# Fixing the order of TensorE, VectorE and ScalarE in a sliding-window attention

## The chip, the cores and the metric

The kernel runs on one core of one Trainium2 chip. The metric is the device time of one execution in microseconds (us); lower is better. The runs of one kernel agree within 1.5%. A profile covers one execution. Engine names: PE is TensorE, DVE is VectorE, ACT is ScalarE, POOL is GpSimd.

## The reference, cut to what matters

One transformer block on 2048 tokens of width 512: a modulated LayerNorm, attention with 32 heads of width 16 in which a query sees the 256 keys up to its own, an output projection, two more LayerNorms, and an MLP across tokens.

```python
mask = (idx[:, None] - idx[None, :] >= 0) & (idx[:, None] - idx[None, :] < W)   # W = 256
scores = jnp.where(mask[None, None], scores, -1000000000.0)
p = _softmax(scores, axis=-1)
o = jnp.einsum('bhqk,bhkd->bhqd', p, v)
...
h = _layernorm(x, axis=-1) * (1 + ca) + sa
x = x + ga * _A_ref(h, A_wqkv, A_wo)          # attention
h = _layernorm(x, axis=-1) * (1 + cb) + sb
x = x + gb * _B_ref(h, B_w1, B_b1, B_w2, B_b2)   # MLP across tokens
```

## The kernel before

Tokens are handled in four groups of 512, and the heads of a group in four units of 8. A unit has five chunks (four in group 0). A chunk is: scores on PE into `pss`, one exp on ACT from `pss` to `et`, two mask multiplications on DVE, then the value sums on PE: `pox` collects the weighted values, `poy` the normalisers. After a unit's last chunk ACT computes 1/poy as exp(-ln(poy)), and DVE scales: `OT = pox * lz`. There are 76 chunks in all. Beside them runs "dense" work: the projections of the next group, the output projection and LayerNorms of the previous group, and in groups 2 and 3 the first halves ("partials") of MLP sums.

The tiles into which PE writes its results are in PSUM, and the program has few of them. `pss` (128 x 2048) exists once, so the next scores wait for this exp (7.0 us in 14 waits of the profiled run). `pox` and `poy` exist once each, so a new unit's first value sums wait for the scaling of the unit before (up to 1.2 us at a time there). Dense jobs share two buffers of 128 x 512 (`ps_d`). To copy a result out of PSUM is called an eviction here; it is done by DVE, or by ACT as a "side job" beside its exps. In the profiled run one of 128 x 512 took 0.68 us on DVE (`kb`, mean) and 0.58 to 0.60 us on ACT (`QT`).

```python
    ps_d = ctx.enter_context(tc.tile_pool(name="ps_d", bufs=2, space=PSUM))
    ps_s = ctx.enter_context(tc.tile_pool(name="ps_s", bufs=1, space=PSUM))
    ps_o = ctx.enter_context(tc.tile_pool(name="ps_o", bufs=1, space=PSUM))
    ...
    def emit_norm(u):
        lz = work.tile([P, D], F32, name="lz", tag="lz", bufs=2)
        nc.scalar.activation(out=lz[:], in_=u.y[:], func=ACT.Ln)
        nc.scalar.activation(out=lz[:], in_=lz[:], func=ACT.Exp, scale=-1.0)
        nc.vector.tensor_tensor(out=OT[u.G % 2][u.g8][:], in0=u.x[:], in1=lz[:], op=ALU.mult)
    ...
        et = emit_exp_mask(tiles, ch, mk)
        if i + 1 < len(steps):
            v = steps[i + 1][0]
            tiles = emit_scores(v.G, v.g8, steps[i + 1][2])
        pend.append((u, ci, ch, et))
        credit += per_step
        while bg and credit >= 1.0:          # dense jobs of this chunk
            bg.pop(0)()
            credit -= 1.0
        while len(pend) > (1 if i + 1 < len(steps) else 0):
            pu, pci, pch, pet = pend.pop(0)
            emit_av(pu, pci, pch, pet, pci == 4)
            if pci == 4:
                emit_norm(pu)
```

This is only the order in which the program is written. A scheduler puts each engine's instructions into another order at build time. The order that each engine then ran is read from the profiles.

The softmax here doesn't subtract the row's maximum and nothing guards it: scores larger than these inputs give would overflow.

## Time and profile before

The median is 333.14 us (332.96 to 334.24, three runs). The profiled run took 331.52 us.

| part of the profiled run (span 329.7 us) | us |
|---|---|
| start of the 1st and of the 2nd exp | 24.65, 32.62 |
| group 0, from its 2nd exp | 38.8 |
| groups 1, 2, 3 | 55.2, 55.7, 53.3 |
| end of the last exp | 235.6 |
| from there to the end (MLP) | 94.1 |
| time in the attention at half clock (2 us windows) | 10 |

The group times are differences of exp starts in the ScalarE timeline; the last group ends with its last exp. The half-clock time is the missing clock summed over windows of 2 us and doubled, since 0.50 is the lowest clock that any of these windows shows.

The page of the profile, with busy time and share of each engine, then the busy tenths of PE in 40 slices, the granted clock in tenths, and the shares of the chain of waits:

```profile
PE 256.8 (78%) x3269; PEld 125.8 (38%) x3313; DVE 227.3 (69%) x517; ACT 182.6 (55%) x165; POOL 34.8 (11%) x68
...
PE   0588888987876756986789796888873899999973
...
PEclk9999999999999995899999999999997899999999
...
PE 37%; DVE 35%; ACT 15%; DMA 8%; issue 3%; SPq 1%; another core or an unknown queue 0%; DVEq 0%; ACTq 0%
```

No engine is saturated (PE, the busiest, has 78%), and the chain passes from one engine to another. Whoever wants to gain time here has to shorten waits, not work.

The list of waits (who waited for whom: us in total, times, longest):

```profile
ACT et L413 <- PE pss L401: 34.6, 49, 1.6
...
PE pox L465 <- DVE et L425: 13.3, 21, 1.3
...
PE pox L465 <- DVE OT_1_147 L478: 1.6, 2, 1.2
```

ACT loses 34.6 us waiting for scores. PE waits 13.3 us in one of the groups for masks before value sums. Waits of `pox` for a scaling `OT` are small: the one shown is the largest of eight groups, and the eight sum to 5.2 us.

The timeline, in order of start (start, duration, engine, line, operation; in brackets the idle time before and its end):

```profile
113.98 1.88 ACT L413 ACTIVATE et<-pss 128x2048 bf16<-128x2048 f32 x1 [0.50 <-PE pss L401]
...
115.76 0.59 ACT L476 ACTIVATE lz<-poy 128x512 f32<-128x512 f32 x1
...
116.38 0.63 ACT L477 ACTIVATE lz<-lz 128x512 f32<-128x512 f32 x1
...
116.92 1.86 ACT L413 ACTIVATE et<-pss 128x2048 bf16<-128x2048 f32 x1
117.04 0.69 DVE L478 TENSOR_TENSOR OT_2_152<-pox,lz 128x512 bf16<-128x512 f32 x1
...
117.78 0.41 PE L465 MATMUL pox<-et,VT_143 128*32 128x192 bf16 x12 [0.22 <-DVE OT_2_152 L478]
...
119.27 1.88 ACT L413 ACTIVATE et<-pss 128x2048 bf16<-128x2048 f32 x1 [0.50 <-PE pss L401]
...
121.20 0.40 PE L401 MATMUL pss<-QT_3_130,KT_3_138 32*128 32x192 bf16 x8 [1.12 <-ACT et L413]
...
121.65 1.88 ACT L413 ACTIVATE et<-pss 128x2048 bf16<-128x2048 f32 x1 [0.50 <-PE pss L401]
...
123.58 0.40 PE L401 MATMUL pss<-QT_3_130,KT_3_138 32*128 32x128 bf16 x12 [1.26 <-ACT et L413]
```

Two steady rhythms are seen. Between plain chunks, exps start 2.38 us apart (119.27 to 121.65): 1.88 us of exp, then 0.50 us in which PE makes the next scores. Where ACT also makes a normaliser it is 2.94 us (113.98 to 116.92). There DVE does the scaling at 117.04, as soon as the normaliser is there.

Windows of 4 us (length, then busy time of PE, PEld, DVE, ACT, POOL, each with its count; granted clock, DMA share, GB/s):

```profile
120.00:124.00 4.00, 1.53 (x40) 0.94 (x37) 1.07 (x4) 3.03 (x2) 0.00 (x0) 1.00 0.00 0
124.00:128.00 4.00, 2.38 (x52) 1.44 (x53) 0.81 (x3) 3.26 (x2) 0.00 (x0) 0.55 0.00 0
```

From 120 us there is no dense work and PE is busy 1.53 of 4 us. After that the granted clock falls: 0.55 in the window from 124 us, and 0.50 in the 2 us windows from 126 to 134 us. In the 8 us ahead of the fall PE had no gap above 1.26 us: low activity without a long gap came before it.

### The profile page before, as it was taken

To read this page: it belongs to the slowest core of one execution; us is meant where nothing else is said; L and a number is where in the kernel's file an instruction comes from. 1 tells how busy PE (TensorE), PEld (TensorE's weight loads), DVE (VectorE), ACT (ScalarE), POOL (GpSimd) and SP (SyncE) were. 2 spreads that over 40 slices of the span, in tenths; PEclk is the share of its full clock that TensorE was granted. 3 is DMA by queue.
4 is the path that set the end of the run, shared out by engine and by line. 5 is a ranking of instruction groups with operands and counts; after the bars stand their busy time and mean duration, and the time that the engine had idled before them with its cause. 6 is when DMAs were issued, how large, how long until landed. Compare 5 with 4: busy or idle time off the path is not lost.

```text
span 329.7 us, 7582 instructions
## 1 busy us (share of the span) xinstructions
PE 256.8 (78%) x3269; PEld 125.8 (38%) x3313; DVE 227.3 (69%) x517; ACT 182.6 (55%) x165; POOL 34.8 (11%) x68
## 2 busy tenths in 40 slices
PE   0588888987876756986789796888873899999973
PEld 0353435343543423453344343433331344444431
DVE  7999988648899543899955689644387476535433
ACT  1014797987868788786888876878602353000000
POOL 8403101230101400020230000000000000000000
PEclk9999999999999995899999999999997899999999
DMA  7992039300000000000002202222200991110110
GB/s 219 336 334 6 3 85 287 79 2 0 4 2 2 2 2 2 2 2 1 2 2 66 66 2 66 64 67 66 67 0 10 398 412 73 51 48 34 62 34 32
DMA packets 31434, 24.62 MB, mean 75 GB/s; under 512 B 6056, under 2 KB 29608, under 8 KB 31400
## 3 DMA queue, kind: packets, MB, share of 16 engines
q1 hardware_dynamic: 30336, 23.08, 22.8%
q10 hardware_dynamic: 1064, 1.05, 1.1%
q8 instruction: 26, 0.43, 0.5%
q14 instruction: 8, 0.07, 0.1%
HBM read 22.03 MB, written 2.10 MB: 73 GB/s over the span
## 4 chain that ended last, share of the span: by engine, by line
PE 37%; DVE 35%; ACT 15%; DMA 8%; issue 3%; SPq 1%; another core or an unknown queue 0%; DVEq 0%; ACTq 0%
ACT et L413 11%; DVE st L243 6%; PE pu_4802 L649 4%; PE pu_4645 L649 4%; PE pu L442 4%; DVE et L420 4%; PE pss L401 3%; PE pox L465 3%; DVE et L425 3%; PE pu_4257 L592 2%; DMA x_73<-in_A_x_dram 2%; DMA wqkv<-in_A_wqkv_dram 2%; PE pu_4484 L592 2%; DMA b2b<-in_B_b_dram 2%; DVE VT_143 L336 2%
## 5 line engine op out<-in xcount | busy, mean ns | idle before, releaser
L413 ACT ACTIVATE et<-pss 128x2048 bf16<-128x2048 f32 (+1 forms) x76 | 140.6, 1851 | 35.2 <-PE pss L401 34.6
L465 PE MATMUL poy<-et,ones_bd 128*32 128x128 bf16 (+4 forms) x768 | 42.9, 256 | 4.7 <-DVE et L420 3.5
L420 DVE TENSOR_TENSOR et<-et,maskt 128x256 bf16<-128x256 bf16 (+2 forms) x104 | 32.9, 338 | 9.9 <-ACT et L413 9.6
L649 PEld LDWEIGHTS <-w2r 128*128 128x128 bf16 x224 | 21.9, 98 | 29.6 <-issue 3.7
L425 DVE TENSOR_TENSOR et<-et,maskt 128x512 bf16<-128x512 bf16 x48 | 21.0, 438 | 16.2 <-ACT et L413 16.0
L465 PE MATMUL pox<-et,VT_143 128*32 128x320 bf16 (+4 forms) x352 | 18.4, 255 | 9.3 <-DVE et L425 4.3
L465 PEld LDWEIGHTS <-ones_bd 128*32 128x32 bf16 x768 | 20.4, 97 | 8.3 <-DVE et L420 7.3
L326 PE MATMUL pv<-wqkv,h1T 128*64 128x256 bf16 x256 | 19.3, 277 | 1.1 <-DVE KT_0_131 L306 0.5
L291 PE MATMUL pq<-h1T,wqkv 128*128 128x512 bf16 x56 | 17.4, 393 | 2.3 <-DVE h1T L280 1.0
L465 PEld LDWEIGHTS <-VT_143 128*32 128x32 bf16 x352 | 11.4, 94 | 17.6 <-issue 16.5
L246 ACT ACTIVATE rs<-mv,eps_t 128x4 f32<-128x4 f32 x12 | 3.6, 297 | 26.1 <-DVE mv L244 26.1
L617 ACT ACTIVATE g<-a,b1FM 128x512 bf16<-128x512 f32 x14 | 9.7, 717 | 14.8 <-DVE a L615 14.8
L465 PE MATMUL pox<-et,VT_144 128*32 128x320 bf16 (+4 forms) x208 | 11.3, 264 | 7.3 <-DVE et L425 4.6
L300 PE MATMUL pk<-h1T,wqkv 128*128 128x512 bf16 x57 | 15.9, 391 | 1.3 <-DVE kb L312 0.6
L465 PE MATMUL pox<-et,VT_145 128*32 128x320 bf16 (+4 forms) x208 | 10.7, 256 | 6.6 <-DVE et L425 4.3
L326 PEld LDWEIGHTS <-h1T 128*64 128x64 bf16 x256 | 13.0, 109 | 6.7 <-issue 4.1
L312 DVE CAST kb<-pk 128x512 bf16<-128x512 f32 x15 | 10.2, 682 | 5.8 <-PE pk L300 3.0
L465 PEld LDWEIGHTS <-VT_144 128*32 128x32 bf16 x208 | 7.2, 98 | 11.8 <-issue 11.0
L336 DVE CAST VT_143<-pv 64x512 bf16<-64x512 f32 x16 | 11.0, 687 | 0.3
L465 PEld LDWEIGHTS <-VT_145 128*32 128x32 bf16 x208 | 6.9, 96 | 10.8 <-issue 9.9
L477 ACT ACTIVATE lz<-lz 128x512 f32<-128x512 f32 x16 | 10.1, 631 | 0.4
L476 ACT ACTIVATE lz<-poy 128x512 f32<-128x512 f32 x16 | 9.5, 594 | 1.3 <-PE poy L465 1.3
(622 smaller groups left out, 518.6 us busy)
## 6 DMA issues: line engine op xcount, KB each, us to landing
w2r<-in_B_w_dram SPq DMA_DIRECT2D x14, 512.0 KB, 9.1
wmod<-in_w_mod_dram SPq DMA_DIRECT2D x4, 512.0 KB, 6.9
out_dram<-otile SPq DMA_DIRECT2D x16, 128.0 KB, 1.7
wmod<-in_w_mod_dram ACTq DMA_DIRECT2D x2, 512.0 KB, 6.0
wqkv<-in_A_wqkv_dram SPq DMA_DIRECT2D x2, 384.0 KB, 6.7
wqkv<-in_A_wqkv_dram SPq DMA_DIRECT2D x1, 512.0 KB, 7.6
wod<-in_A_wo_dram SPq DMA_DIRECT2D x1, 512.0 KB, 8.6
w1p_1208<-in_B_w_dram SPq DMA_DIRECT2D x1, 512.0 KB, 4.3
```

The source lines that it names most:

```text
L243: nc.vector.bn_stats(out=st[:], in_=t[:])
L291: nc.tensor.matmul(pq[:], lhsT=wqkv[:, dc, g8 * P : (g8 + 1) * P], rhs=h1T[:, dc, :], start=(dc == 0), stop=(dc == ND - 1),)
L300: nc.tensor.matmul(pk[:], lhsT=wqkv[:, dc, D + g8 * P : D + (g8 + 1) * P], rhs=h1T[:, dc, :], start=(dc == 0), stop=(dc == ND - 1),)
L326: nc.tensor.matmul(pv[KB * par : KB * (par + 1), i, :].rearrange("p (a d) -> p a d", d=DH), lhsT=h1T[:, dc, tok], rhs=wv[:, dc, par, :, :] ...
L336: nc.vector.tensor_copy(out=dst, in_=src)
L413: nc.scalar.activation(out=et[:, :, lo:D], in_=tiles[:, :, lo:D], func=ACT.Exp, scale=SCORE_SCALE,)
L420: nc.vector.tensor_tensor(out=dst, in0=dst, in1=msk.to_broadcast([P, 4, KB * mn]), op=ALU.mult,)
L425: nc.vector.tensor_tensor(out=dst, in0=dst, in1=maskt[:, m0 : m0 + 2, :].unsqueeze(1).to_broadcast([P, 4, 2, KB]), op=ALU.mult,)
L442: nc.tensor.matmul(pu[:], lhsT=w1s(sc, fc), rhs=hb[sc][:], start=(sc == 0), stop=(sc == 7),)
L465: nc.tensor.matmul(dst[32 * j : 32 * j + 32, KB * qs : KB * (qs + nq)], lhsT=VT[r][:, kbi, 4 * u.g8 + j, :] if isv else ones_bd[:], rhs=et ...
L592: nc.tensor.matmul(ftiles[fc], lhsT=w1s(sc, fc), rhs=hb[sc][:], start=(sc == 8), stop=(sc == NT - 1), skip_group_check=True,)
L649: nc.tensor.matmul(ftiles[100 + t], lhsT=w2r[:, fc, t * P : (t + 1) * P], rhs=guT[fc][:], start=(fc == 0), stop=(fc == NF - 1), skip_group ...
```

## The change

The intent is a software pipeline that the scheduler may not disturb. Three thin wrappers mark ("pin") the instructions of PE, DVE and ACT in the attention loop, dense work included, as "keep in program order". The written order of a chunk becomes: exp, ScalarE side jobs, masks, next scores, dense work, value sums of the chunk before. Dense work is dealt out by "streams" that follow the share of the group that is done. LayerNorm jobs are cut into smaller pieces. The diff, cut to its core (the comments at the right are added here):

```diff
+    class Ordered:
...
+            def wrapped(*args, **kwargs):
+                ins = call(*args, **kwargs)
+                if pinned[0]:
+                    tc.keep_in_program_order(ins)
+                return ins
...
+    te, ve, ac = Ordered(nc.tensor), Ordered(nc.vector), Ordered(nc.scalar)
...
     def emit_norm(u):
         lz = work.tile([P, D], F32, name="lz", tag="lz", bufs=2)
-        nc.scalar.activation(out=lz[:], in_=u.y[:], func=ACT.Ln)
-        nc.scalar.activation(out=lz[:], in_=lz[:], func=ACT.Exp, scale=-1.0)
-        nc.vector.tensor_tensor(out=OT[u.G % 2][u.g8][:], in0=u.x[:], in1=lz[:], op=ALU.mult)
+        ac.activation(out=lz[:], in_=u.y[:], func=ACT.Ln)
+        ac.activation(out=lz[:], in_=lz[:], func=ACT.Exp, scale=-1.0)
+        return lambda: ve.tensor_tensor(
+            out=OT[u.G % 2][u.g8][:], in0=u.x[:], in1=lz[:], op=ALU.mult,
+        )
...
+            if G > 0:
+                streams.append(Stream(0.15, 0.7 if G == 2 else 1.0, post_work(G - 1)))
+            if G + 1 < NG:
+                streams.append(Stream(0.0, 1.0, proj_work(G + 1)))
...
+        et = emit_exp(pss, ch)
+        flush_later()                                       # ScalarE side jobs
+        scale = emit_norm(norm_due) if norm_due else None
+        norm_due = None
+        emit_mask(et, mk)
+        if not last:
             v = steps[i + 1][0]
-            tiles = emit_scores(v.G, v.g8, steps[i + 1][2])
+            pss = emit_scores(v.G, v.g8, steps[i + 1][2])
+        share = (i - step0) / (nsteps - 2)
+        for st in streams:                                  # dense work
+            st.run(share)
+        if scale:
+            scale()                                         # DVE: scaling of the unit before
         pend.append((u, ci, ch, et))
...                                                         # value sums of the chunk before
```

More of the change, by code (lines that the diff above doesn't have):

```diff
@@ L83, with __init__, __getattr__ @@
     F32 = DT.float32
+    pinned = [False]
+    class Ordered:
+        def __init__(self, engine):
+            self.engine = engine
+        def __getattr__(self, name):
+            call = getattr(self.engine, name)
+            def wrapped(*args, **kwargs):
[3 more added lines that the diff above has]
+                return ins
+            return wrapped
+    te, ve, ac = Ordered(nc.tensor), Ordered(nc.vector), Ordered(nc.scalar)
     nc.scalar.preload_act_table_set("natural_log_exp_and_others")
@@ L193, in emit_mod_fm @@
                 for k in range(ND):
-                    nc.tensor.matmul(
+                    te.matmul(
                         ps_fm[:, col : col + 1],
@@ L199, in emit_mod_fm @@
                     )
-        nc.vector.tensor_copy(out=modFM[:, 0:4], in_=ps_fm[:, 0:4])
-        nc.vector.tensor_scalar_add(out=modFM[:, 4:8], in0=ps_fm[:, 4:8], scalar1=1.0)
+        ve.tensor_copy(out=modFM[:, 0:4], in_=ps_fm[:, 0:4])
+        ve.tensor_scalar_add(out=modFM[:, 4:8], in0=ps_fm[:, 4:8], scalar1=1.0)
     def emit_mod_bc(v, dst, add1):
@@ L205, in emit_mod_bc @@
         for k in range(ND):
-            nc.tensor.matmul(
+            te.matmul(
                 ps_b[:], lhsT=sT_rep[:, k, :], rhs=wmod[:, k, v * D : (v + 1) * D],
@@ L210, in emit_mod_bc @@
         if v == 2:
-            nc.vector.tensor_scalar(
+            ve.tensor_scalar(
                 out=dst[:], in0=ps_b[:], scalar1=ZSCALE, scalar2=0.0, op0=ALU.mult, op1=ALU.add,
@@ L214, in emit_mod_bc @@
         elif add1:
-            nc.vector.tensor_scalar_add(out=dst[:], in0=ps_b[:], scalar1=1.0)
+            ve.tensor_scalar_add(out=dst[:], in0=ps_b[:], scalar1=1.0)
         else:
-            nc.vector.tensor_copy(out=dst[:], in_=ps_b[:])
+            ve.tensor_copy(out=dst[:], in_=ps_b[:])
     def emit_masks():
@@ L235, in emit_masks, with on_act, __init__, add @@
                 nc.gpsimd.tensor_copy(out=maskt[rows, 2 + i, :], in_=tmpm[rows, half, 1, :])
-    def ln_stats(tiles, tag):
-        n = len(tiles)
-        mv = small.tile([P, 4, nc.vector.BN_AGGR_DIM], F32, name="mv", tag=tag + "mv")
-        for i, t in enumerate(tiles):
-            st = small.tile([P, nc.vector.BN_STATS_DIM], F32, name="st", tag=tag + "st")
-            nc.vector.bn_stats(out=st[:], in_=t[:])
-            nc.vector.bn_aggr(out=mv[:, i, :], in_=st[:])
-        rs = small.tile([P, 4], F32, name="rs", tag=tag + "rs")
-        nc.scalar.activation(out=rs[:, 0:n], in_=mv[:, 0:n, 1], func=ACT.Ln, bias=eps_t[:], scale=1.0)
-        nc.scalar.activation(out=rs[:, 0:n], in_=rs[:, 0:n], func=ACT.Exp, scale=-0.5)
-        return mv, rs
-    def normalize(dst, src, mv, rs, i):
-        nc.vector.tensor_scalar(
+    later = []
+    def on_act(job):
+        if pinned[0]:
+            later.append(job)
+        else:
+            job()
+    class Norm:
+        def __init__(self, tag, n=4):
+            self.tag, self.n, self.got = tag, n, 0
+            self.mv = small.tile([P, n, nc.vector.BN_AGGR_DIM], F32, name="mv", tag=tag + "mv")
+            self.rs = small.tile([P, n], F32, name="rs", tag=tag + "rs")
+        def add(self, t):
+            st = small.tile([P, nc.vector.BN_STATS_DIM], F32, name="st", tag=self.tag + "st")
+            ve.bn_stats(out=st[:], in_=t[:])
+            ve.bn_aggr(out=self.mv[:, self.got, :], in_=st[:])
+            self.got += 1
+        def close(self):
+            def job():
+                ac.activation(
+                    out=self.rs[:], in_=self.mv[:, :, 1], func=ACT.Ln, bias=eps_t[:], scale=1.0,
+                )
+                ac.activation(out=self.rs[:], in_=self.rs[:], func=ACT.Exp, scale=-0.5)
+            on_act(job)
+    def normalize(dst, src, norm, i):
+        mv, rs = norm.mv, norm.rs
+        ve.tensor_scalar(
             out=dst, in0=src, scalar1=mv[:, i, 0:1], scalar2=rs[:, i : i + 1],
@@ L260, in proj_work, with ln1_stats, ln1 @@
         xn = []
-        def ln1():
-            mv, rs = ln_stats([xres[4 * G + i] for i in range(4)], "l1")
-            for i in range(4):
-                t = wpool.tile([P, D], BF, name="xn", tag="xn", bufs=5)
-                normalize(t[:], xres[4 * G + i][:], mv, rs, i)
-                xn.append(t)
-        work_list.append(ln1)
+        norm = Norm("l1")
+        def ln1_stats(i):
+            norm.add(xres[4 * G + i])
+            if i == 3:
+                norm.close()
+        def ln1(i):
+            t = wpool.tile([P, D], BF, name="xn", tag="xn", bufs=5)
+            normalize(t[:], xres[4 * G + i][:], norm, i)
+            xn.append(t)
+        for i in range(4):
+            work_list.append((0.8, lambda i=i: ln1_stats(i)))
+        work_list.append(None)
+        for i in range(4):
+            work_list.append((0.4, lambda i=i: ln1(i)))
         def tr(dp):
@@ L274, in tr @@
                     dc = 2 * dp + i
-                    nc.tensor.transpose(
+                    te.transpose(
                         pt[:, i, tl * P : (tl + 1) * P], xn[tl][:, dc * P : (dc + 1) * P], identity[:]
@@ L279, in tr @@
                 dc = 2 * dp + i
-                nc.vector.tensor_scalar(
+                ve.tensor_scalar(
                     out=h1T[:, dc, :], in0=pt[:, i, :],
@@ L285, in proj_work @@
         for dp in range(2):
-            work_list.append(lambda dp=dp: tr(dp))
+            work_list.append((1.0, lambda dp=dp: tr(dp)))
         def q(g8):
@@ L290, in q @@
             for dc in range(ND):
-                nc.tensor.matmul(
+                te.matmul(
                     pq[:], lhsT=wqkv[:, dc, g8 * P : (g8 + 1) * P], rhs=h1T[:, dc, :],
@@ L294, in q @@
                 )
-            nc.scalar.activation(out=QT[r2][g8][:], in_=pq[:], func=ACT.Copy)
+            on_act(lambda: ac.activation(out=QT[r2][g8][:], in_=pq[:], func=ACT.Copy))
         def k(g8):
@@ L299, in k @@
             for dc in range(ND):
-                nc.tensor.matmul(
+                te.matmul(
                     pk[:], lhsT=wqkv[:, dc, D + g8 * P : D + (g8 + 1) * P], rhs=h1T[:, dc, :],
@@ L305, in k @@
                 for par in range(2):
-                    nc.vector.tensor_scalar(
+                    ve.tensor_scalar(
                         out=KT[r3][g8][:, :, par, :], in0=pk[:].rearrange("p (b k) -> p b k", k=KB),
@@ L311, in k @@
             kb = work.tile([P, D], BF, name="kb", tag="kb", bufs=2)
-            nc.vector.tensor_copy(out=kb[:], in_=pk[:])
+            ve.tensor_copy(out=kb[:], in_=pk[:])
             for par in range(2):
@@ L325, in v @@
                     for par in range(2):
-                        nc.tensor.matmul(
+                        te.matmul(
                             pv[KB * par : KB * (par + 1), i, :].rearrange("p (a d) -> p a d", d=DH),
@@ L335, in v @@
                 dst = VT[r3][rows, 2 * tb : 2 * tb + 2, :, par * DH : (par + 1) * DH]
-                nc.vector.tensor_copy(out=dst, in_=src)
-        work_list.append(lambda: q(0))
-        work_list.append(lambda: k(0))
+                ve.tensor_copy(out=dst, in_=src)
+        work_list.append((1.0, lambda: q(0)))
+        work_list.append((1.0, lambda: k(0)))
         for tb in range(4):
-            work_list.append(lambda tb=tb: v(tb))
+            work_list.append((1.2, lambda tb=tb: v(tb)))
         for g8 in range(1, ND):
-            work_list.append(lambda g8=g8: q(g8))
-            work_list.append(lambda g8=g8: k(g8))
+            work_list.append((1.0, lambda g8=g8: q(g8)))
+            work_list.append((1.0, lambda g8=g8: k(g8)))
         return work_list
@@ L356, in wo @@
             for g in range(ND):
-                nc.tensor.matmul(
+                te.matmul(
                     pa[:], lhsT=OT[r2][g][:, tl * P : (tl + 1) * P], rhs=wod[:, g, :],
@@ L360, in wo, with ln2_stats, ln3_stats, ln3 @@
                 )
-            nc.vector.tensor_tensor(out=xres[tb][:], in0=pa[:], in1=xres[tb][:], op=ALU.add)
-        def ln2():
-            st["a"] = ln_stats([xres[4 * G + i] for i in range(4)], "l2")
+            ve.tensor_tensor(out=xres[tb][:], in0=pa[:], in1=xres[tb][:], op=ALU.add)
         h2 = []
+        def ln2_stats(i):
+            if i == 0:
+                st["a"] = Norm("l2")
+            st["a"].add(xres[4 * G + i])
+            if i == 3:
+                st["a"].close()
         def mod2(i):
-            mv, rs = st["a"]
             t = work.tile([P, D], BF, name="xn2", tag="xn2", bufs=2)
-            normalize(t[:], xres[4 * G + i][:], mv, rs, i)
+            normalize(t[:], xres[4 * G + i][:], st["a"], i)
             u = work.tile([P, D], BF, name="h2", tag="h2", bufs=4)
-            nc.vector.tensor_tensor(out=u[:], in0=t[:], in1=bc_cb1[:], op=ALU.mult)
-            nc.vector.tensor_tensor(out=u[:], in0=u[:], in1=bc_sb[:], op=ALU.add)
+            ve.tensor_tensor(out=u[:], in0=t[:], in1=bc_cb1[:], op=ALU.mult)
+            ve.tensor_tensor(out=u[:], in0=u[:], in1=bc_sb[:], op=ALU.add)
             h2.append(u)
-        def ln3():
-            mv, rs = ln_stats(h2, "l3")
-            for i in range(4):
-                normalize(hb[4 * G + i][:], h2[i][:], mv, rs, i)
+        def ln3_stats(i):
+            if i == 0:
+                st["b"] = Norm("l3")
+            st["b"].add(h2[i])
+            if i == 3:
+                st["b"].close()
+        def ln3(i):
+            normalize(hb[4 * G + i][:], h2[i][:], st["b"], i)
         for tl in range(4):
-            work_list.append(lambda tl=tl: wo(tl))
-        work_list.append(ln2)
+            work_list.append((0.9, lambda tl=tl: wo(tl)))
         for i in range(4):
-            work_list.append(lambda i=i: mod2(i))
-        work_list.append(ln3)
+            work_list.append((0.8, lambda i=i: ln2_stats(i)))
+        work_list.append(None)
+        for i in range(4):
+            work_list.append((1.0, lambda i=i: mod2(i)))
+        for i in range(4):
+            work_list.append((0.8, lambda i=i: ln3_stats(i)))
+        work_list.append(None)
+        for i in range(4):
+            work_list.append((0.4, lambda i=i: ln3(i)))
         return work_list
@@ L400, in emit_scores @@
                 rows = slice(32 * j, 32 * j + 32)
-                nc.tensor.matmul(
+                te.matmul(
                     pss[:, j, col : col + KB * nq],
@@ L408, in emit_scores, with emit_exp, emit_mask @@
         return pss
-    def emit_exp_mask(tiles, ch, masks):
+    def emit_exp(pss, ch):
         lo = min(p[3] for p in ch)
         et = epool.tile([P, 4, D], BF, name="et")
-        nc.scalar.activation(
-            out=et[:, :, lo:D], in_=tiles[:, :, lo:D], func=ACT.Exp, scale=SCORE_SCALE,
-        )
+        ac.activation(out=et[:, :, lo:D], in_=pss[:, :, lo:D], func=ACT.Exp, scale=SCORE_SCALE)
+        return et
+    def emit_mask(et, masks):
         for col, stride, m0, mn in masks:
@@ L419, in emit_exp_mask @@
                 msk = maskt[:, m0 : m0 + mn, :].rearrange("p m k -> p (m k)").unsqueeze(1)
-                nc.vector.tensor_tensor(
+                ve.tensor_tensor(
                     out=dst, in0=dst, in1=msk.to_broadcast([P, 4, KB * mn]), op=ALU.mult,
@@ L424, in emit_exp_mask @@
                 dst = et[:, :, col : col + 2 * stride].rearrange("p j (m s) -> p j m s", s=stride)[:, :, :, 0:KB]
-                nc.vector.tensor_tensor(
+                ve.tensor_tensor(
                     out=dst, in0=dst,
@@ L428, in emit_exp_mask @@
                 )
-        return et
     def load_w1(pair, half):
@@ L441, in partial @@
         for sc in range(8):
-            nc.tensor.matmul(
+            te.matmul(
                 pu[:], lhsT=w1s(sc, fc), rhs=hb[sc][:], start=(sc == 0), stop=(sc == 7),
@@ L446, in partial @@
         t = pool.tile([P, D], F32, name=f"part{fc}")
-        nc.vector.tensor_copy(out=t[:], in_=pu[:])
+        ve.tensor_copy(out=t[:], in_=pu[:])
         part[fc] = t
@@ L464, in emit_av @@
                 for j in range(4):
-                    nc.tensor.matmul(
+                    te.matmul(
                         dst[32 * j : 32 * j + 32, KB * qs : KB * (qs + nq)],
@@ L475, in emit_norm @@
         lz = work.tile([P, D], F32, name="lz", tag="lz", bufs=2)
-        nc.scalar.activation(out=lz[:], in_=u.y[:], func=ACT.Ln)
-        nc.scalar.activation(out=lz[:], in_=lz[:], func=ACT.Exp, scale=-1.0)
-        nc.vector.tensor_tensor(out=OT[u.G % 2][u.g8][:], in0=u.x[:], in1=lz[:], op=ALU.mult)
+        ac.activation(out=lz[:], in_=u.y[:], func=ACT.Ln)
+        ac.activation(out=lz[:], in_=lz[:], func=ACT.Exp, scale=-1.0)
+        return lambda: ve.tensor_tensor(
+            out=OT[u.G % 2][u.g8][:], in0=u.x[:], in1=lz[:], op=ALU.mult,
+        )
     nc.vector.memset(VT[0][:], 0.0)
     pw = proj_work(0)
-    pw[0]()
+    pw = [w for w in pw if w]
+    for _, w in pw[:8]:
+        w()
     emit_mod_fm()
-    for w in pw[1:]:
+    for _, w in pw[8:]:
         w()
@@ L489, in early @@
     def early():
-        nc.vector.tensor_copy(out=b1FM[:], in_=b1b[:])
-        nc.vector.tensor_copy(out=b2FM[:], in_=b2b[:])
+        ve.tensor_copy(out=b1FM[:], in_=b1b[:])
+        ve.tensor_copy(out=b2FM[:], in_=b2b[:])
     def wod_scale():
-        nc.vector.tensor_tensor(
+        ve.tensor_tensor(
             out=wod[:], in0=wod[:], in1=bc_ga[:].unsqueeze(1).to_broadcast([P, ND, D]), op=ALU.mult,
@@ L516, with __init__, run, flush_later @@
                 steps.append((u, ci, ch, mk))
-    bg = []
+    class Stream:
+        def __init__(self, lo, hi, jobs):
+            self.lo, self.hi, self.jobs = lo, hi, list(jobs)
+            self.total = sum(j[0] for j in jobs if j)
+            self.done = 0.0
+        def run(self, share):
+            while self.jobs:
+                if self.jobs[0] is None:
+                    self.jobs.pop(0)
+                    return
+                cost, w = self.jobs[0]
+                if self.lo + (self.hi - self.lo) * (self.done + cost / 2) / self.total > share:
+                    return
+                self.done += cost
+                self.jobs.pop(0)
+                w()
+    def flush_later():
+        while later:
+            later.pop(0)()
+    streams = []
     done_group = -1
-    per_step = 0.0
-    credit = 0.0
+    step0 = nsteps = 0
     pend = []
-    tiles = emit_scores(steps[0][0].G, steps[0][0].g8, steps[0][2])
+    norm_due = None
+    pss = emit_scores(steps[0][0].G, steps[0][0].g8, steps[0][2])
+    pinned[0] = True
     for i, (u, ci, ch, mk) in enumerate(steps):
         if u.G != done_group:
-            for w in bg:
-                w()
-            if u.G == 1:
+            while any(st.jobs for st in streams):
+                flush_later()
+                for st in streams:
+                    st.run(2.0)
+            flush_later()
+            G = done_group = u.G
+            if G == 1:
                 modw.release()
@@ L533 @@
                     load_w1(pair, 0)
-            if u.G == 3:
+            if G == 3:
                 wpool.release()
                 partB = ctx.enter_context(tc.tile_pool(name="partB", bufs=1, side="right"))
-            done_group = u.G
-            bg = []
-            post = post_work(u.G - 1) if u.G > 0 else mod_jobs + [early, wod_scale] + zero_jobs[8:]
-            proj = proj_work(u.G + 1) if u.G + 1 < NG else []
-            n = max(len(post), len(proj))
-            bg = proj[:1]
-            rest = proj[1:]
@@ L544 @@
-            while post or rest:
-                if post:
-                    bg.append(post.pop(0))
-                if rest:
-                    bg.append(rest.pop(0))
-            if u.G == 0:
-                bg = zero_jobs[:8] + bg
-            if u.G == 2:
-                bg += [lambda fc=fc: partial(fc) for fc in range(4)]
-            if u.G == 3:
-                bg += [lambda fc=fc: partial(fc) for fc in range(4, NF)]
-            nsteps = sum(1 for s in steps if s[0].G == u.G)
-            per_step = len(bg) / (nsteps - 2)
@@ L557 @@
-            credit = -per_step
-        et = emit_exp_mask(tiles, ch, mk)
-        if i + 1 < len(steps):
-            v = steps[i + 1][0]
-            tiles = emit_scores(v.G, v.g8, steps[i + 1][2])
-        pend.append((u, ci, ch, et))
-        credit += per_step
-        while bg and credit >= 1.0:
-            bg.pop(0)()
-            credit -= 1.0
-        while len(pend) > (1 if i + 1 < len(steps) else 0):
+            streams = []
+            if G == 0:
+                streams.append(Stream(0.0, 0.3, [(1.0, w) for w in zero_jobs[:8]]))
+                streams.append(Stream(0.3, 1.0, [(1.0, w) for w in mod_jobs + [early, wod_scale]]))
@@ new lines @@
+            if G == 1:
+                streams.append(Stream(0.0, 0.5, [(1.0, w) for w in zero_jobs[8:]]))
+            if G > 0:
+                streams.append(Stream(0.15, 0.7 if G == 2 else 1.0, post_work(G - 1)))
+            if G + 1 < NG:
+                streams.append(Stream(0.0, 1.0, proj_work(G + 1)))
+            if G == 2:
+                streams.append(Stream(0.7, 1.0, [(1.0, lambda fc=fc: partial(fc)) for fc in range(4)]))
+            if G == 3:
+                streams.append(Stream(0.0, 1.0, [(1.0, lambda fc=fc: partial(fc)) for fc in range(4, NF)]))
@@ new lines @@
+            step0 = i
+            nsteps = sum(1 for s in steps if s[0].G == G)
+        last = i + 1 == len(steps)
+        et = emit_exp(pss, ch)
+        flush_later()
+        scale = emit_norm(norm_due) if norm_due else None
+        norm_due = None
+        emit_mask(et, mk)
+        if not last:
+            v = steps[i + 1][0]
+            pss = emit_scores(v.G, v.g8, steps[i + 1][2])
+        share = (i - step0) / (nsteps - 2)
+        for st in streams:
+            st.run(share)
+        if scale:
+            scale()
@@ L568 @@
+        pend.append((u, ci, ch, et))
+        while len(pend) > (0 if last else 1):
             pu, pci, pch, pet = pend.pop(0)
@@ L570 @@
             if pci == 4:
-                emit_norm(pu)
-    for w in bg:
-        w()
+                norm_due = pu
+    while any(st.jobs for st in streams):
+        flush_later()
+        for st in streams:
+            st.run(2.0)
+    flush_later()
+    emit_norm(norm_due)()
+    pinned[0] = False
     ftiles = {}
@@ L595, in mlp1 @@
                 )
-    pw = post_work(NG - 1)
+    pw = [w for w in post_work(NG - 1) if w]
     first = list(range(6))
     f_tiles([("s", [0, 1, 2, 3]), ("x", [4]), ("y", [5])])
-    for w in pw:
+    for _, w in pw:
         w()
```

## The prediction

> **What bounds it now.** From the page: PE 78%, DVE 69%, ACT 55% busy of 329.7 us; the chain of waits is mixed (PE 37%, DVE 35%, ACT 15%), its largest line the attention's exp (11%). Nothing is saturated. From the timeline of ScalarE: the 76 exps run from 24.65 to 235.6 us, then a 94 us tail (MLP) that the change leaves alone. One score buffer ties exp and scores together: in quiet stretches exp starts are 2.38 us apart (exp 1.88 plus 0.50 waiting for the next scores), with the two normaliser activations 2.94. Groups of 4 heads-blocks take 46.8, 55.2, 55.7, 53.3 us, where 2.38/2.94 alone would give about 50 for each of the last three. So at most some 13 us can be won there, plus 1 us in the prologue (LayerNorm statistics that stand between VectorE's first evictions go away).
>
> **What changes.** No arithmetic is added or removed. The scheduler's freely interleaved order becomes fixed: PE does scores, the whole dense job(s), then value sums of the chunk before; DVE does masks, all dense evictions, and only then the scaling of the finished unit; ScalarE side jobs follow an exp.[...]
>
> Gains: value sums no longer wait for their own masks (wait groups pox/poy after et: about 24 us of PE idle, mostly not critical); ScalarE side jobs fall into the 0.5 us score gap.
>
> Losses, costed per chunk with durations of this trace (scores+value sums 1.0 us of PE, a dense job 0.87, V projection 0.95, a partial of 8 matmuls 1.74; DVE: masks 0.56 to 0.70, eviction 0.61, V eviction 1.22, LN modulation 1.0, statistics 0.67):
> - The next scores come after all of that on PE. Chunks with one dense job fit in 2.38; with a partial 2.8, with q or k plus a partial 3.65, two output projections plus transposes over 4. In the old order such work was split across chunks. I count some 10 us.
> - pox is single buffered: the first value sums of the next unit wait for the scaling, which now stands behind that chunk's dense evictions (masks 0.6, dense 0.9 to 1.7, evictions 0.6 to 1.2, modulation 1.0, then 0.61). Instead of about 1.9 us after the exp it comes after 2.7 to 4.6, and PE, with the next scores behind it, stands still. 16 units: some 13 us.
> - Group boundaries hold 5 to 6 chunks with no dense work, twice. At 120 to 124 us PE was 38% busy and the granted clock fell to 0.50 at 126 to 134[...]. I expect two such dips: 2 to 3 us.
>
> Adding this up chunk by chunk puts the last exp near 253 us rather than 235.6; such a tally is pessimistic about slack and says nothing of balance that the author may have tuned on the chip, so I shrink it.
>
> **Prediction:** 343 us, range 322 to 357. Faster by over 2%: 0.23; within 2%: 0.23; slower by over 2%: 0.54.
>
> **Signs.** Right: exp-to-exp gaps of 3 to 5 us at the unit boundaries; PE pox waiting for OT (DVE), clearly more than now; PE masks waits gone; groups 1 to 3 at 56 to 62 us each; clock 0.5 near both group boundaries; tail still 94 us. Wrong: exp starts 2.4 to 2.9 apart nearly everywhere, groups near 50 us.
>
> **What would make it wrong.** If VectorE has drained its evictions earlier than I count, the scaling is not late and the pinned pipeline runs at the ScalarE limit, near 320. If partials overlap more, group 3 gains.

The losses named are some 10, some 13 and 2 to 3 us, 25 to 26 us together before the gains, and the tally chunk by chunk came to 253 us for the last exp, 17.4 us after the 235.6 of before. That a late item on DVE holds up what stands behind it was at this point the author's assumption; the profile after shows one such place, with 5.00 us of PE idle.

## The result, and the profile after

The changed kernel takes 364.56 us (median of 4, 361.94 to 366.16) against 333.55 us of the kernel before in the same session. The ratio is 1.0921, 95% interval 1.0844 to 1.0998. Here and below a ratio is the mean time of one kernel's runs over that of the other's of the same rounds, so it is not quite the ratio of the quoted medians. The output is correct. The change is 9% slower.

| part of the profiled run | before | after |
|---|---|---|
| start of the 2nd exp | 32.62 | 31.33 |
| group 0, from its 2nd exp | 38.8 | 44.7 |
| group 1 | 55.2 | 61.3 |
| group 2 | 55.7 | 69.7 |
| group 3 | 53.3 | 59.8 |
| end of the last exp | 235.6 | 266.8 |
| from there to the end | 94.1 | 94.9 |
| time in the attention at half clock | 10 | 68 |

Nearly all of the loss lies in the attention: 31.2 us of the 32.0 us between the two profiled runs. The same four lines of the page:

```profile
PE 267.9 (74%) x3313; PEld 127.2 (35%) x3313; DVE 233.6 (65%) x517; ACT 183.6 (51%) x165; POOL 33.5 (9%) x68
...
PE   0685797956783974859299757876688599999984
...
PEclk9998598985999797598769989998999699999999
...
PE 53%; DVE 25%; ACT 18%; issue 2%; DMA 1%; SPq 0%; DVEq 0%
```

PE's busy share falls, and the clock line shows many dips where the attention had one. The chain of waits moves to PE (53%). The waits:

```profile
ACT et L96 <- PE pss L96: 60.5, 51, 7.1
PE pox L96 <- DVE OT L96: 34.2, 15, 6.9
```

`pox` now waits 34.2 us for the scaling, 15 times and up to 6.9 us. ACT waits 60.5 us for scores instead of 34.6. The waits of value sums for masks are gone from the list, as the change intended.

The timeline around a unit boundary of group 1:

```profile
110.77 0.63 ACT L96 ACTIVATE lz<-lz 128x512 f32<-128x512 f32 x1
111.11 1.39 DVE L96 CAST VT<-pv 64x512 bf16<-64x512 f32 x2
111.31 1.86 ACT L96 ACTIVATE et<-pss 128x2048 bf16<-128x2048 f32 x1
112.51 0.76 DVE L96 TENSOR_TENSOR et<-et,maskt 128x768 bf16<-128x768 bf16 x2
113.19 0.41 DVE L96 TENSOR_SCALAR xn<-x,mv,rs 128x512 bf16<-128x512 bf16 x1
113.63 0.43 DVE L96 TENSOR_TENSOR h<-xn,bc_cb 128x512 bf16<-128x512 bf16 x1
114.09 0.43 DVE L96 TENSOR_TENSOR h<-h,bc_sb 128x512 bf16<-128x512 bf16 x1
114.53 1.39 DVE L96 CAST VT<-pv 64x512 bf16<-64x512 f32 x2
115.95 0.69 DVE L96 TENSOR_TENSOR OT<-pox,lz 128x512 bf16<-128x512 f32 x1
...
116.70 0.35 PE L96 MATMUL pox<-et,VT 128*32 128x192 bf16 x4 [5.00 <-DVE OT L96]
...
117.67 0.62 PE L96 MATMUL pss<-QT,KT 32*128 32x192 bf16 x8
...
118.34 1.88 ACT L96 ACTIVATE et<-pss 128x2048 bf16<-128x2048 f32 x1 [5.17 <-PE pss L96]
```

The two normaliser activations end at about 111.4, so the scaling could run then. But it stands in DVE's list behind the eviction of the chunk before (111.11), the masks (112.51), three modulation operations (113.19 to 114.5) and two more evictions (114.53). It starts at 115.95. PE stands for 5.00 us in front of the first value sums, and the next scores stand behind those in PE's list, although they need nothing from the scaling. So the next exp starts 7.03 us after this one.

Another place, in group 2, shows a chunk with too much dense work:

```profile
188.41 0.40 PE L96 MATMUL pss<-QT,KT 32*128 32x192 bf16 x12
...
188.74 1.04 PE L96 MATMUL pk<-h1T,wqkv 128*128 128x512 bf16 x4
188.86 1.88 ACT L96 ACTIVATE et<-pss 128x2048 bf16<-128x2048 f32 x1
...
189.62 1.89 PE L96 MATMUL pu<-hb,w1p 128*128 128x512 bf16 x8
...
191.44 0.27 PE L96 MATMUL pox<-et,VT 128*32 128x192 bf16 x4
...
191.99 0.40 PE L96 MATMUL pss<-QT,KT 32*128 32x128 bf16 x12
...
192.44 1.88 ACT L96 ACTIVATE et<-pss 128x2048 bf16<-128x2048 f32 x1 [1.70 <-PE pss L96]
```

The k projection and a whole partial stand between the scores at 188.41 and the next scores at 191.99. ACT was done at 190.74 (188.86 plus 1.88) and idles until 192.44.

Windows of 4 us, two at the start of group 1 and two at the boundary shown above:

```profile
76.00:80.00 4.00, 1.91 (x52) 1.22 (x53) 0.82 (x3) 3.47 (x2) 1.33 (x2) 0.78 1.21 290
80.00:84.00 4.00, 2.08 (x40) 0.93 (x39) 2.90 (x8) 3.17 (x4) 0.00 (x0) 0.50 0.93 224
112.00:116.00 4.00, 0.00 (x0) 0.00 (x0) 3.86 (x9) 1.17 (x1) 0.00 (x0) 0.98 0.00 0
116.00:120.00 4.00, 3.30 (x48) 1.98 (x48) 2.35 (x6) 1.66 (x1) 0.00 (x0) 0.50 0.00 0
```

At 76 us the chunks have no dense work, PE is busy 1.91 of 4 us and the clock falls (0.78, then 0.50). At 112 us PE stands still for the whole window, waiting for the scaling, and the clock falls too (0.98, then 0.50). In both cases the next matmuls take longer: groups of eight score matmuls at 80.33 and 117.67 us took 0.61 and 0.62 us, and 0.40 us at 110.30 us, where the clock was 1.00. The longest gap of PE before the first of these dips:

```profile
77.96 0.40 PE L96 MATMUL pss<-QT,KT 32*128 32x128 bf16 x12 [1.43 <-ACT et L96]
```

### The profile page after: what moved, and what is told of

Read it like the earlier page. It is cut to its first block, busy times and chain, and to the rows that moved or that the text cites. A ratio compares the mean times of both kernels' runs of the same rounds, so it can differ in the third digit from the quotient of the medians.

```text
span 361.7 us, 7615 instructions
## 1 busy us (share of the span) xinstructions
PE 267.9 (74%) x3313; PEld 127.2 (35%) x3313; DVE 233.6 (65%) x517; ACT 183.6 (51%) x165; POOL 33.5 (9%) x68
## 4 chain that ended last, share of the span: by engine, by line
PE 53%; DVE 25%; ACT 18%; issue 2%; DMA 1%; SPq 0%; DVEq 0%
ACT et L96 17%; PE pu L753 14%; PE pu L96 8%; PE pss L96 7%; PE pu L696 5%; PE pox L96 4%; DVE VT L96 4%; PE pa L96 4%; DVE st L96 4%; PE poy L96 3%; DVE OT L96 2%; DVE et L96 2%; DVE h L96 2%; PE pq L96 2%; PE pk L96 2%
## 5 line engine op out<-in xcount | busy, mean ns | idle before, releaser
L96 ACT ACTIVATE et<-pss 128x2048 bf16<-128x2048 f32 (+1 forms) x76 | 140.6, 1850 | 60.7 <-PE pss L96 60.5
L96 DVE TENSOR_TENSOR et<-et,maskt 128x256 bf16<-128x256 bf16 (+2 forms) x152 | 50.8, 376 | 32.9 <-ACT et L96 32.3
L96 PE MATMUL pox<-et,VT 128*32 128x128 bf16 (+4 forms) x768 | 44.1, 281 | 34.3 <-DVE OT L96 34.2
L96 PE MATMUL pss<-QT,KT 32*128 32x128 bf16 (+4 forms) x768 | 34.8, 275 | 31.5 <-ACT et L96 31.4
L753 PE MATMUL pu<-guT,w2r 128*128 128x512 bf16 x224 | 49.5, 379 | 2.5 <-DVE o L736 2.5
L96 PEld LDWEIGHTS <-VT 128*32 128x32 bf16 x768 | 20.9, 104 | 61.2 <-DVE OT L96 33.1
L364 POOL TENSOR_SCALAR KT<-kb,mask_par 128x512 bf16<-128x512 bf16 x30 | 22.5, 761 | 172.2 <-DVE kb L96 172.2
L696 PE MATMUL pu<-hb,w1p 128*128 128x512 bf16 x112 | 27.9, 406 | 6.5 <-DVE hb L96 5.7
L753 PEld LDWEIGHTS <-w2r 128*128 128x128 bf16 x224 | 21.8, 98 | 29.7 <-issue 3.7
L96 PE MATMUL pu<-hb,w1p 128*128 128x512 bf16 x112 | 28.8, 403 | 0.0
L96 DVE CAST VT<-pv 64x512 bf16<-64x512 f32 x32 | 22.0, 687 | 6.1 <-PE pv L96 5.7
L96 DVE BATCH_NORM_STATS2 st<-x 128x6 f32<-128x512 bf16 x32 | 21.5, 676 | 0.7 <-DMA x<-in_A_x_dram 0.7
L96 PE MATMUL pa<-wod,OT 128*128 128x512 bf16 x64 | 18.4, 427 | 0.0
```

The source lines that it names most:

```text
L96: ins = call(*args, **kwargs)
L364: nc.gpsimd.tensor_scalar(out=KT[r3][g8][:, :, par, :], in0=kb[:].rearrange("p (b k) -> p b k", k=KB), scalar1=mask_par[:, par : par + 1], ...
L696: nc.tensor.matmul(ftiles[fc], lhsT=w1s(sc, fc), rhs=hb[sc][:], start=(sc == 8), stop=(sc == NT - 1), skip_group_check=True,)
L753: nc.tensor.matmul(ftiles[100 + t], lhsT=w2r[:, fc, t * P : (t + 1) * P], rhs=guT[fc][:], start=(fc == 0), stop=(fc == NF - 1), skip_group ...
```

## The experiments

Theory A: the loss comes from the late place of one DVE operation, the scaling. Theory B: it comes from the lowered clock, in quiet chunks and after stalls. Theory C: it comes from whole dense jobs that do not fit into one exp. Rivals: the new division of the dense work, or in-order execution as such, costs the time. All ten runs gave correct results. A summary:

| run | edit | median us | ratio to before | last exp ends | `pox` waits for OT |
|---|---|---|---|---|---|
| changed kernel | | 364.56 | 1.092 | 266.8 | 34.2 |
| e1_scale_early | scaling right after the masks | 346.59 | 1.041 | 251.9 | 14.2 |
| e2_warm | idle matmuls in quiet chunks | 355.22 | 1.068 | 258.4 | 31.8 |
| e3_early_warm | both | 340.53 | 1.024 | 244.4 | 11.6 |
| e4_unpin | nothing pinned | 335.06 | 1.007 | 240.9 | 6.3 |
| e5_spread | e3, dense work by a table | 319.11 | 0.960 | 223.3 | 3.9 |
| e6_spread_no_idle | e5 without idle matmuls | 323.59 | 0.973 | 227.4 | 4.9 |
| e7_free_vector | DVE not pinned | 346.19 | 1.044 | 253.6 | 18.0 |
| e8_pin_vector_only | only DVE pinned | 343.36 | 1.032 | 246.2 | 3.6 |
| e9_spread_late | e5, scaling late again | 348.80 | 1.046 | 252.6 | 31.4 |
| e10_spread_unpinned | e5, nothing pinned | 329.16 | 0.988 | 232.7 | 4.5 |

The last two columns come from the one profiled run of each kernel, which for e7 was its slowest (350.66 us).

### e1_scale_early

```diff
         emit_mask(et, mk)
+        if scale:
+            scale()
         if not last:
...
             st.run(share)
-        if scale:
-            scale()
```

> The changed kernel, with one VectorE operation per unit moved: the scaling of a finished unit (OT) stands right after the masks instead of behind the chunk's dense evictions. Theory A (late scaling: PE stands 34 us in 15 waits of pox for OT): those waits fall to under 12 us, the longest from 6.9 to about 2 us, and the time falls by 13 to 20 us, to 345 to 352 us. Theory B (whole dense jobs and the lowered clock of quiet chunks cost the time; the wait for OT only shows where PE idles anyway): under 6 us gained, 359 us or more.

Measured: 346.59 us, so 18.0 us less than the changed kernel, inside what theory A expected. Its waits:

```profile
ACT et L96 <- PE pss L96: 40.9, 49, 2.9
...
PE pox L96 <- DVE OT L96: 14.2, 10, 3.7
```

Two lines moved within the written order are worth 18 us. The waits for the scaling fell by 20.0 us, to 14.2 rather than below 12, and the longest is 3.7 us rather than 2. One place that still loses time: the normaliser is ready at 167.4 us, and ACT then waits 2.91 us for scores, so that the exp after the one at 167.32 starts at 172.09. The clock is hardly mended: 54.5 us at half clock, after 68.

### e2_warm

The edit, cut, with comments added:

```diff
+        seen = npe[0]                      # count of PE instructions so far
         for st in streams:
             st.run(share)
+        if npe[0] == seen and not last:    # no dense PE work in this chunk
+            idle = ps_d.tile([P, D], F32, name="idle", tag="psd")
+            for _ in range(8):
+                te.matmul(idle[:, 0 : 4 * KB], lhsT=identity[:],
+                          rhs=maskt[:].rearrange("p m k -> p (m k)"), start=True, stop=True, ...)
```

> The changed kernel plus eight idle matmuls of 256 columns (result never read) in each chunk that has no dense PE work, to keep PE active there. Theory B: the granted clock in the attention rises from 0.86 to above 0.93 and 6 to 12 us are gained, 353 to 359 us. Theory A: the stalls at pox remain 30 us or more and lower the clock by themselves; gain under 5 us.

Measured: 355.22 us, 9.3 us less, inside what theory B expected. The granted clock in the attention rose from 0.86 to 0.95, and the time at half clock fell from 68 to 24 us. The clock line of the page and the waits:

```profile
PEclk9999999999996989998679999999999699999999
```

```profile
ACT et L100 <- PE pss L100: 53.1, 49, 7.2
...
PE pox L100 <- DVE OT L100: 31.8, 15, 7.0
```

The stalls at `pox` stay (31.8 us). So the lowered clock in quiet chunks is a cost of its own. The dips that are left lie at stalls, for example after 108 and 170 us (the exps at 114.12 and 177.82 us come after 5.17 and 7.18 us of waiting, and the clock is 0.50 from 110 to 116 and from 172 to 180 us). Added work without any use made the kernel faster, by these 9.3 us.

### e3_early_warm

> Both edits. If the two causes are separate, the gains add: 335 to 345 us. If the clock falls because of the stalls, this is within 4 us of the early scaling alone.

The edit is both of the above. Measured: 340.53 us, 24.0 us less than the changed kernel; the separate gains sum to 27.3. They nearly add, so the two causes are mostly separate; the 3.3 us between the sums is less than the spread of the changed kernel's own runs (361.94 to 366.16 us). The time at half clock adds as well: 68 us in the changed kernel, 54.5 in e1, 24 in e2, 10 here, as in the kernel before. So the idle matmuls take away 44 us of it with or without the late scaling, and the early scaling 14 us. Against the kernel before 2.4% are still missing. Fourteen exp-to-exp distances are still above 3.2 us; the largest are 5.37, 5.23, 5.13 and 5.12 us.

### e4_unpin

```diff
-    pinned[0] = True
+    pinned[0] = False
```

> The changed kernel's new written order, but nothing pinned: the scheduler may reorder again. Theory that the pinning is the cost: back to 330 to 340 us, with waits of pox for OT under 12 us. Rival, that the new division and spread of the dense work is the cost: still above 355 us.

Measured: 335.06 us, ratio to before 1.0069 (1.0020 to 1.0117). With the same written order, but free to reorder, the scheduler undoes nearly all of the loss. So the new division and spread of the dense work is not the cause by itself; it costs only together with the pinning.

### e5_spread

The pinned order of e3, with a table in place of the streams, and each partial cut into two jobs of four matmuls; the memsets of POOL are written at the start of groups 0 and 1 instead of spread. One letter is the next job of a queue, which can be as small as one LayerNorm statistic: P projections, O output and LayerNorms, M modulation, A a half partial.

```diff
+PLAN = [
+    ["PPP", "P", "PPPP", "P", "P", "PM", "P", "P", "P", "PP", "M", "P", "P", "MP", "MP", "MMPP"],
+    ["PPP", "P", "POP", "O", "PPO", "P", "OPO", "PO", "OOP", "P", "O", "OOP", "P", "OO", "O", "P", "OPP", "OP", "OOPPO", "OP"],
+    ["PPP", "P", "O", "PPPOPO", "POO", "OP", "OPP", "OP", "OP", "P", "P", "OOOPO", "P", "OOP", "OPP", "OOOOP", "AA", "AA", "AA", "AA"],
+    ["A", "AA", "AO", "O", "O", "A", "OAOO", "A", "AO", "AO", "OA", "AOOA", "OA", "AOOO", "A", "A", "AOA", "AOO", "O", "OA"],
+]
-        share = (i - step0) / (nsteps - 2)
-        for st in streams:
-            st.run(share)
+        for name in PLAN[u.G][i - step0]:
+            streams[name].pop(0)()
```

The table was found by trying many and adding up, queue by queue, the durations seen in the traces.

> Pinned order as in the run with early scaling and idle matmuls (340.5 us), but the dense jobs are dealt to chunks by a fixed table so that PE and VectorE work of one chunk fits its exp: at most one dense job in most chunks, two where the normaliser runs, and the partials cut into two halves of four matmuls. Theory C (what is left over before, some 8 us, are chunks whose dense work is longer than the exp): 9 to 19 us less than 340.5, 321 to 331 us, faster than the kernel before; few exp-to-exp distances above 3.2 us (14 there). Rival (in-order execution itself costs, semaphores and latency between engines): under 4 us gained, 336 us or more.

Measured: 319.11 us, ratio to before 0.9603 (0.9561 to 0.9645): 21.4 us less than e3, and 4% faster than the kernel before. That is better than theory C expected (9 to 19 us gained, 321 to 331 us). The last exp ends at 223.3 us. Groups 1 to 3 take 50.5, 53.2 and 49.9 us, and only two distances are above 3.2 us. The clock line and the waits:

```profile
PEclk9999999999999999999999999999995999999999
```

```profile
ACT et L108 <- PE pss L108: 23.1, 44, 0.8
...
PE pox L108 <- DVE OT L108: 3.9, 5, 1.4
```

The one dip left is in the MLP. ACT's wait for scores is 23.1 us, no longer than 0.8 us at a time; 60.5 in the changed kernel, 34.6 before. The rival, that in-order execution itself is the cost, falls. How the gain divides between the table and the halved partials was not tested.

### e6_spread_no_idle

Edit: the same table, no idle matmuls.

> The same table without the idle matmuls. If quiet chunks alone lower the clock: dips come back where the table leaves 2 to 4 chunks without dense work (starts of groups), and 2 to 6 us are lost against the run with them. If the dips came from stalls only: within 1.5 us.

Measured: 323.59 us, 4.5 us more than e5, inside the expected 2 to 6, and 24 us at half clock in the attention against none. The quiet chunks cost this even where there is hardly a stall. Half clock is not all lost time: 24 us of it cost 4.5 us here, and the 44 us that e2 removed cost 9.3, so about a fifth in both (an estimate from these two pairs).

### e7_free_vector and e8_pin_vector_only

```diff
-                if pinned[0]:
+                if pinned[0] and self.engine is not nc.vector:    # e7; e8: "is nc.vector"
```

> The changed kernel with PE and ScalarE pinned as written and VectorE left to the scheduler, which moves the scaling of a unit ahead of evictions. If the late scaling on VectorE is the main cost of pinning: about as good as the early scaling, 340 to 350 us. If pinning PE in whole jobs is the main cost: 355 us or more.

> The changed kernel with only VectorE pinned as written; PE and ScalarE free. If the written VectorE order is the main cost: it stays above 348 us although PE may be rearranged. If PE's order is: 333 to 342 us, like nothing pinned (335).

Measured: 346.19 and 343.36 us. Freeing DVE alone gives 18.4 us, as much as moving the scaling by hand. Freeing PE and ACT together gives 21.2 us, and the waits of `pox` for OT fall to 3.6 us. The expectations for e8 both missed (above 348, or 333 to 342): it lies between. A reading that fits both runs: the bad place of the scaling hurts because both lists are fixed. It is late on DVE, and PE has no other work ahead of it while it is awaited. Freedom on either side mends a large part, and only both together (e4) give 335. PE and ACT were not freed apart from each other, and e7 still waits 18.0 us for OT, and e7 and e8 still have 58 and 41 us at half clock in the windows up to 226 us.

### e9_spread_late and e10_spread_unpinned

Edits to e5: the scaling behind the dense work again; and nothing pinned.

> The table kernel (319 us) with the scaling of a unit put back behind the chunk's dense work, as the change had it. Theory A, that the place of this one VectorE operation costs by itself, whatever the spread: adding up the queues gives 20 us or more (the table puts two dense jobs into the normaliser chunks): 335 to 345 us, pox waits for OT of 25 us or more. If the late scaling only hurt through the uneven dense work: under 6 us, 325 us or less.

> The table kernel with nothing pinned: the scheduler reorders the table. If pinning is worth something once the written order is balanced: 326 to 338 us, near the kernel before. If the table alone does it and the scheduler keeps its spread: 317 to 322 us.

Measured: 348.80 us, above the 335 to 345 expected, and 329.16 us, inside its 326 to 338. The waits of e9:

```profile
ACT et L108 <- PE pss L108: 53.3, 50, 5.1
PE pox L108 <- DVE OT L108: 31.4, 15, 5.5
```

The late scaling costs 29.7 us in the balanced kernel, more than the expected 16 to 26 and more than the 18.0 us in the changed one. It again makes dips: 31 us at half clock. So its place counts by itself, not only through uneven dense work. And pinning is worth 10.0 us for this table, which without it takes 329.16 us. Idle matmuls in the kernel before, unchanged otherwise, were not tried.

## Why the prediction was right or wrong

The prediction said 343 us, range 322 to 357, slower by over 2% the likeliest. The direction was right. The size was wrong: 364.56 us lies above the range.

- "pox is single buffered ... 16 units: some 13 us." The mechanism was right: 34.2 us of waits; moving the scaling is worth 18.0 us in e1, and 14.7 us from e2 to e3, where idle matmuls hold up the clock. The term was somewhat small.
- "The next scores come after all of that on PE ... I count some 10 us." Right in kind: the chunks over 3.2 us that were left in e3 went away with the table. The 21.4 us of e5 is no measure of this term alone, since the table also goes below the kernel before.
- "Group boundaries hold 5 to 6 chunks with no dense work, twice ... I expect two such dips: 2 to 3 us." **This is the step that failed.** The mechanism at the boundaries was right, but the cost was too small by a factor of three or more: the idle matmuls of e2 alone regained 9.3 us, and they left 24 us at half clock. The time at half clock was 68 us, and not some two dips on top of the one before with its 10 us. Dips came in group 0 (clock 0.50 from 34 to 44 us), at the boundaries (80 to 90 us), and after stalls for the scaling (116 to 122 us), which the prediction had not connected with the clock. Together the scaling and the clock cost 24.0 us (e3), where these two terms had 15 to 16.
- "Adding this up chunk by chunk puts the last exp near 253 us ... so I shrink it." The sum was 13.8 us short of the 266.8 us measured. **Shrinking it is the second step that failed**, and went the wrong way: 253 is 17.4 us behind the 235.6 of before, which on top of 333 would have been about 350, inside the stated range, but still 14 us below the measured time. The hope that the streams were balanced on the chip had no number behind it.
- "groups 1 to 3 at 56 to 62 us each": 61.3, 69.7 and 59.8. Group 2 is out; it has the most dense work, and the longest stall (an exp-to-exp distance of 8.95 us).
- "PE masks waits gone", "tail still 94 us" (94.9), "plus 1 us in the prologue" (the second exp starts 1.29 us earlier, though the first starts 4.73 us later, at 29.38): right.
- "At most some 13 us can be won there": e5 wins 12.3 us up to the end of the last exp (223.3 against 235.6), close to that figure; one kernel does not show that it is a bound. It was the changed kernel's order that did not reach it.

One thing stays open: what the whole dense jobs alone cost. e3 is about 8 us above the kernel before, where the prediction had some 10 us for this term, but no run changes only the size of the jobs in the changed kernel.

## What to carry to other kernels

When you pin an order, you take over every queue position: look on each engine for the operation that another engine's whole list waits for (here the scaling that frees a single PSUM buffer; its place was worth 18.0 us in e1), and put it ahead of work that nobody waits for. Then add up each engine's work per pipeline step, and deal the background work so that each step fits. In these runs a step too full held up the next scores (ACT idle for 1.70 us before 192.44 us in the changed kernel), and where steps were too empty the PE clock fell (0.50 after the quiet chunks at 76 us; idle matmuls in such chunks brought the mean in the attention from 0.86 to 0.95 in e2); a well-dealt fixed order then beat both the scheduler's order of before (by 4%, or 2.7% without idle matmuls) and the scheduler's version of itself (by 10 us).
